# Fourteen like products ahead of the first transposes, two reordered steps, and V's low part split over two places

## The chip, the cores and the metric

The kernel runs on one core of one Trainium2 chip. The metric is the device time of one execution in microseconds. Before the change the median of three runs is 637.38 us (637.07 to 637.69). The profile shows one further execution of 637.08 us, whose span from the first to the last instruction is 635.3 us.

The engines are called by the profile's short names: PE is TensorE (PEld its weight loads), DVE is VectorE, ACT is ScalarE, POOL is GpSimd, SP is SyncE, which here only issues DMAs. ACTq and SPq are DMA issues on ACT's and SP's instruction streams.

## The reference

Decaying linear attention in blocks of 64 rows, then a channel mixer with a low-rank term over the sequence:

```python
# q, k, v: (4, 8, 768, 64); lam: (8,), between 0.97 and 0.99
for b in range(nb):                                   # attention, block = 64
    intra = einsum('bhic,bhjc->bhij', qb, kb) * Dmask # lam**(i-j), lower triangle
    intra = einsum('bhij,bhjd->bhid', intra, vb)
    inter = einsum('bhid,bhde->bhie', qb * lam_pow, kv_state)
    out[:, :, sl] = intra + inter
    kv_state = lam_block * kv_state + einsum('bhsd,bhse->bhde', kb * rev_pow, vb)
x = out.transpose(0, 2, 1, 3).reshape(B, S, H * D)    # (4, 768, 512)
h = x.transpose(0, 2, 1) @ U @ V                      # U: (768, 32), V: (32, 768), float64 inputs
u = x + h.transpose(0, 2, 1)
out = u + maximum(u @ w_ch1, 0) @ w_ch2               # 512 -> 2048 -> 512
```

The float64 inputs U, V and the two mixer weights reach the kernel as pairs of 32-bit words and are turned into float32 on DVE and ACT in small steps.

## The kernel before, in words

**Tiling.** The sequence is taken in 24 steps of 128 rows, six per batch entry (`NS = 24`, `NT = 6`). All eight heads of a step lie side by side in one 128 x 512 tile. Step s loads q, k and v (256 KB each), transposes q and k with PE (`prep`, L419), multiplies them (`scores`, L466), masks the scores with powers of lam (`masked`, DVE, L475), applies them to v (`intra`, L524), adds the part from the running state (`inter`, L536), and updates the state (`state`: products `pkv`, L489, and a DVE sum into `kv`, L495 to L500). ACT copies the transposes out of PSUM (L425), fades the state (L459) and copies the finished rows out (`take_x`, L546). POOL scales k and q by powers of lam (`ks`, L439; `qs`, L450). After six steps `low` (L556) forms the product with U, and from the eighth step on `mix` (L631), `mixed` (L643) and `turn` (L694) apply V to the rows of the batch entry before and transpose them. This front part takes about 112 us; the mixer's large products fill the rest.

**Order of the work.** Nothing is reordered by a scheduler in the front: `pieces` lists the pieces of every step in the order in which each engine gets its instructions, and each engine runs its own list in order, waiting on semaphores. So an instruction that waits holds up everything behind it on its engine. DMA issues sit in the same lists: q, k and the weights on SP, most v loads on ACT. Conversion steps of U, V and the first weights are strewn between the pieces by `aside(s)`; their ACT instructions are put off to the next `late` piece.

**PSUM.** Banks are taken by tag, one buffer each: "pm", "pqk", "pss", "px". A tile of a tag waits until the tile before it under this tag has been read.

**The opening.** While the first loads are on their way PE runs `keep_busy` products on a tile of zeros (L402): two of 128 x 128, then the product that spreads lam over the partitions (`pl`, L852), then two more of 128 x 128 and nine of 16 x 16. DVE copies `pl` to `lamb`, makes the eight masks by scans (L367), the powers for q by four scans (`powers`, L379), and last copies the mask's final column to `rev` (L857), which POOL needs for `ks`.

**The fourth step (s = 3).** At its end `aside(3)` comes ahead of `masked(4)`. It holds four DVE instructions: the last two of U (L196, L201) and the first two of V (L170, L158). V's two ACT instructions (L177, L178) follow in step 4, after the copies of step 5's transposes and ahead of `take_x(4)`.

**The eighth step (s = 7).** `intra(7)` comes ahead of `state(7)`; the state's products use the tag "pqk". Then `inter(7)`, `mix(0)` under the tag "pm", `scores(8)`, and on DVE `mixed(0)`, which `mix(1)` waits for. In the seventh step `aside(6)` puts both halves of V's low part (L799, 32 x 384 each) on DVE, behind `masked(7)`.

## Time and profile before

| what | value |
|---|---|
| three runs | 637.07, 637.38, 637.69 us |
| the profiled execution, and its span | 637.08 us, 635.3 us |
| PE busy | 627.3 us (99% of the span) |
| DVE, ACT, POOL busy | 467.6, 330.9, 146.9 us |
| DMA rate from 6 to 10 us | 280 to 288 GB/s |

PE is busy almost throughout, so the time is the sum of PE's work plus the few places where PE stands idle or runs slowly. To read the profile for this change one looks at those few places in the first 42 us, and asks in each case what was late.

### The profile page before, as it was taken

To read this page: it belongs to the slowest core of one execution; us is meant where nothing else is said; L and a number is where in the kernel's file an instruction comes from. 1 tells how busy PE (TensorE), PEld (TensorE's weight loads), DVE (VectorE), ACT (ScalarE), POOL (GpSimd) and SP (SyncE) were. 2 spreads that over 40 slices of the span, in tenths; PEclk is the share of its full clock that TensorE was granted. 3 is DMA by queue.
4 is the path that set the end of the run, shared out by engine and by line. 5 is a ranking of instruction groups with operands and counts; after the bars stand their busy time and mean duration, and the time that the engine had idled before them with its cause. 6 is when DMAs were issued, how large, how long until landed. Compare 5 with 4: busy or idle time off the path is not lost.

```text
span 635.3 us, 13669 instructions
## 1 busy us (share of the span) xinstructions
PE 627.3 (99%) x5213; PEld 529.2 (83%) x5213; DVE 467.6 (74%) x752; ACT 330.9 (52%) x604; POOL 146.9 (23%) x125
## 2 busy tenths in 40 slices
PE   9999999999999999999999999999999999999997
PEld 8888989888888888888888888888888888888886
DVE  5776887757888788797888799784665754855844
ACT  4675756546777777778777744332322322323220
POOL 4476878000000000000667500030210300300300
PEclk9999999999999999999999999999999999999999
DMA  9989995348797888755876796363353353542521
GB/s 223 254 215 253 249 247 153 133 166 289 284 348 270 309 292 291 272 199 187 262 231 212 239 323 217 116 232 100 108 208 99 137 195 100 190 128 96 183 84 66
DMA packets 141955, 129.61 MB, mean 204 GB/s; under 512 B 82562, under 2 KB 99970, under 8 KB 141890
## 3 DMA queue, kind: packets, MB, share of 16 engines
q1 hardware_dynamic: 116768, 122.32, 59.6%
q10 hardware_dynamic: 25122, 6.42, 4.5%
q8 instruction: 41, 0.67, 0.4%
q14 instruction: 24, 0.20, 0.1%
HBM read 79.04 MB, written 49.28 MB: 202 GB/s over the span
## 4 chain that ended last, share of the span: by engine, by line
PE 97%; DVE 1%; ACT 1%; DMA 1%; issue 0%; ACTq 0%; DVEq 0%
PE pz L983 24%; PE pz L1343 14%; PE pz L1345 14%; PE pd L1347 14%; PE z L983 5%; PE pss L466 4%; PE px L524 4%; PE p L983 3%; PE pz L911 2%; PE d L983 2%; PE px L536 2%; PE pqk L419 2%; PE c L983 2%; PE pkv L489 1%; PE pd L922 1%; PE pp L556 1%
## 5 line engine op out<-in xcount | busy, mean ns | idle before, releaser
L1319 ACT ACTIVATE m<-rm 128x512 fp32r<-128x512 f32 x96 | 60.6, 631 | 174.0 <-PE pd L1347 131.0
L1324 DVE SCALAR_TENSOR_TENSOR m<-rm,m 128x512 fp32r<-128x512 f32 x96 | 71.6, 747 | 81.0 <-ACT m L1319 81.0
L983 PE MATMUL pz<-u_hl,w 128*128 128x512 f32 x448 | 110.3, 389 | 0.0
L1343 PE MATMUL pz<-w_hl,m 128*128 128x512 f32 x264 | 102.7, 389 | 0.0
L1345 PE MATMUL pz<-w_hl,m 128*128 128x512 f32 x264 | 102.7, 389 | 0.0
L1347 PE MATMUL pd<-w_d,m 128*128 128x512 f32 (+1 forms) x267 | 101.4, 387 | 0.0
L983 PEld LDWEIGHTS pz<-u_hl,w 128*128 128x128 f32 x448 | 84.1, 188 | 17.5
L285 POOL TENSOR_TENSOR w<-w 128x512 fp32r<-128x512 f32 x29 | 40.5, 1414 | 210.8 <-DVE w L279 197.3
L1325 DVE SCALAR_TENSOR_TENSOR m<-m 128x512 fp32r<-128x512 f32 x96 | 74.9, 780 | 3.1
L1375 POOL TENSOR_TENSOR o<-o,u 128x512 f32<-128x512 f32 x20 | 29.8, 1521 | 198.5 <-DVE o L1371 198.5
L983 PE MATMUL pz<-u_d,w 128*128 128x512 f32 x224 | 59.9, 389 | 0.0
L1347 PEld LDWEIGHTS pd<-w_d,m 128*128 128x128 f32 x267 | 49.8, 188 | 10.3
L1345 PEld LDWEIGHTS pz<-w_hl,m 128*128 128x128 f32 x264 | 49.6, 188 | 10.3
L1343 PEld LDWEIGHTS pz<-w_hl,m 128*128 128x128 f32 x264 | 49.6, 188 | 10.2
L983 PEld LDWEIGHTS pz<-u_d,w 128*128 128x128 f32 x224 | 42.0, 188 | 8.7
L1343 PE MATMUL pz<-w,m 128*128 128x512 f32 x120 | 46.7, 389 | 0.0
L1345 PE MATMUL pz<-w,m 128*128 128x512 f32 x120 | 46.7, 389 | 0.0
L1347 PE MATMUL pd<-w,m 128*128 128x512 f32 x120 | 46.7, 389 | 0.0
L990 ACT ACTIVATE pz<-pz 128x512 f32<-128x512 f32 x56 | 32.5, 581 | 26.4 <-PE pz L983 26.4
L475 DVE TENSOR_TENSOR sm<-pss,mask 128x512 f32<-128x512 f32 x48 | 30.9, 685 | 18.7 <-PE pss L466 18.4
L994 ACT ACTIVATE r<-pz 128x512 f32<-128x512 f32 x56 | 33.2, 595 | 12.1 <-PE pz L983 11.4
L196 DVE SCALAR_TENSOR_TENSOR sc<-words,sc 128x512 uint32<-128x512 uint32 (+2 forms) x34 | 23.7, 696 | 18.0 <-ACT sc L178 18.0
(140 smaller groups left out, 1119.8 us busy)
## 6 DMA issues: line engine op xcount, KB each, us to landing
r_d<-r SPq DMA_DIRECT2D x96, 256.0 KB, 2.9
rm<-r_d SPq DMA_DIRECT2D x96, 256.0 KB, 2.6
words<-in_moe_w_ch_dram SPq DMA_DIRECT2D x30, 512.0 KB, 5.1
wf<-forms_d SPq DMA_DIRECT2D x56, 128.0 KB, 2.9
u_d<-x_nat SPq DMA_DIRECT2D x24, 256.0 KB, 3.8
u<-u_d SPq DMA_DIRECT2D x24, 256.0 KB, 4.9
qraw<-in_q_dram SPq DMA_DIRECT2D x23, 256.0 KB, 5.0
out_dram<-o SPq DMA_DIRECT2D x23, 256.0 KB, 2.0
```

Source lines behind the costliest of these rows:

```text
L285: engine.tensor_tensor(out=st["third"], in0=st["low"].bitcast(FP32), in1=st["hi"].bitcast(FP32), op=ALU.subtract,)
L475: nc.vector.tensor_tensor(out=sm[:, x], in0=pss[:, x], in1=mask[:, x], op=ALU.mult)
L983: nc.tensor.matmul(out=out, lhsT=weights, rhs=moving, start=start and i == 0, stop=i == len(pieces) - 1, skip_group_check=not start,)
L990: nc.scalar.mul(acc, acc, 1.0 + E)
L994: nc.scalar.mul(r, acc, 4096.0)
L1319: nc.scalar.activation(out=m[:, 0], in_=rs[i], func=AF.Relu, scale=NEAR)
L1324: nc.vector.scalar_tensor_tensor(m[:, 1], r, 0.0, hi, ALU.max, ALU.subtract)
L1325: nc.vector.scalar_tensor_tensor(m[:, 2], hi, E, low, ALU.mult, ALU.subtract)
L1343: nc.tensor.matmul(out=pz, lhsT=m[:, 0, cols], rhs=hi, start=first, stop=False)
L1345: nc.tensor.matmul(out=pz, lhsT=m[:, 1, cols], rhs=low, start=False, stop=end)
L1347: nc.tensor.matmul(out=pd[:, part], lhsT=m[:, 2, cols], rhs=third[:, part], start=first, stop=end, skip_group_check=part.stop != C,)
L1375: nc.gpsimd.tensor_tensor(out=o, in0=o, in1=u, op=ALU.add)
```

## The change

Four things are edited.

1. The opening: the tile of zeros gets ones in its first row (`ones`) and a second zeroed tile (`rows`, 64 columns) takes lam in its first row by a DVE copy. The product that spreads lam then has the same form as the others: 128 x 128 weights, 64 columns moving. The run is 128, 128, 64 columns, lam's 64, and ten of 56 columns: fourteen products on the same weights.
2. `rev` is copied ahead of `powers`. POOL's first `qs` therefore waits for DVE's `powers` by a semaphore of its own.
3. The fourth step: `aside(3)` comes behind `masked(4)` on DVE.
4. The seventh and eighth step: one half of V's low part moves ahead of `masked(7)` (the new piece `v_low`), the other stays behind it. `state(7)` comes ahead of `intra(7)` and uses the tag "pm", the tag that `mix(0)` takes next.

The order of DMA issues on SP and ACT and the order of instructions on POOL stay as they are, as do all later stages.

```diff
-    def keep_busy(n):
+    def keep_busy(sizes):
         out = two_banks("idle", "pm")[:, 0]
-        for i in range(n):
-            k = P if i < 2 else D // 4
+        for n in sizes:
             nc.tensor.matmul(
-                out=out[0:k, 0:k], lhsT=blank[:, 0:k], rhs=blank[:, 0:k], start=True, stop=True
+                out=out[:, 0:n], lhsT=ones, rhs=ones[:, 0:n], start=True, stop=True
             )
...
-                tag = "pm" if s <= NT else "pss" if c > 1 else "pqk"
+                tag = "pm" if s <= NT + 1 else "pss" if c > 1 else "pqk"
...
-        both = [("intra", s), ("state", s)] 
+        both = [("intra", s), ("state", s)] + [("v_low", s)] * (s == NT)
...
-            step += (both if s > NT else both[::-1]) + [("next_v", s), ("inter", s)]
+            step += (both if s > NT + 1 else both[1:] + both[:1]) + [("next_v", s), ("inter", s)]
...
-        aside_first = 0 < s < NT - 2 or s > NT and c > 0
+        aside_first = 0 < s < NT - 3 or s > NT and c > 0
...
-        def low(g, engine):
-            for out, rows in parts((g,)):
+        def low(g, engine, half=slice(0, 2)):
+            for out, rows in list(parts((g,)))[half]:
...
-            five, lambda: low(3, nc.gpsimd), lambda: low(1, nc.vector),
+            five, lambda: v_low.append(lambda: low(1, nc.vector, slice(0, 1))),
+            lambda: low(3, nc.gpsimd), lambda: low(1, nc.vector, slice(1, 2)),
         ]
+
+    v_low = []
+    run["v_low"] = lambda s: v_low.pop()()
...
-        (v_steps(), (1, 1, 3, 4, 4, 4, 4, 5, 6)),
+        (v_steps(), (1, 1, 3, 4, 4, 4, 4, 5, 5, 6)),
...
-    lam_row = consts.tile([1, H + P], FP32, name="lam_row")
-    blank = x_pool.tile([P, C], FP32, tag="x", name="blank")[:, 0:P]
-    nc.vector.memset(blank, 0.0)
-    nc.vector.memset(lam_row[:, H:], 1.0)
+    lam_row = consts.tile([1, H], FP32, name="lam_row")
+    ones = x_pool.tile([P, C], FP32, tag="x", name="ones")[:, 0:P]
+    rows = x_pool.tile([P, C], FP32, tag="x", name="rows")[:, 0:D]
+    nc.vector.memset(ones, 0.0)
+    nc.vector.memset(ones[0:1], 1.0)
+    nc.vector.memset(rows, 0.0)
...
-    pl = two_banks("pl", "pss")[:, 0, 0:H]
-    keep_busy(2)
-    nc.tensor.matmul(out=pl, lhsT=lam_row[:, H:], rhs=lam_row[:, 0:H], start=True, stop=True)
-    keep_busy(3 + 8)
-    nc.vector.tensor_copy(out=lamb, in_=pl)
+    pl = two_banks("pl", "pss")[:, 0, 0:D]
+    keep_busy([P, P, D])
+    nc.vector.tensor_copy(out=rows[0:1, 0:H], in_=lam_row)
+    nc.tensor.matmul(out=pl, lhsT=ones, rhs=rows, start=True, stop=True)
+    keep_busy([56] * 10)
+    nc.vector.tensor_copy(out=lamb, in_=pl[:, 0:H])
     constants()
+    nc.vector.tensor_copy(out=rev, in_=mask[:, :, :, P - 1])
     powers()
-    nc.vector.tensor_copy(out=rev, in_=mask[:, :, :, P - 1])
```

More of the change, by code (lines that the diff above doesn't have):

```diff
@@ L835 @@
     ordered.enter_context(tc.manual_schedule())
-    lam_row = consts.tile([1, H + P], FP32, name="lam_row")
-    blank = x_pool.tile([P, C], FP32, tag="x", name="blank")[:, 0:P]
-    nc.vector.memset(blank, 0.0)
-    nc.vector.memset(lam_row[:, H:], 1.0)
+    lam_row = consts.tile([1, H], FP32, name="lam_row")
[4 more added lines that the diff above has]
+    nc.vector.memset(rows, 0.0)
     set_ends(vp[:, S + C : S + C + 2].bitcast(FP32))
-    nc.scalar.dma_start(out=lam_row[:, 0:H], in_=lam.unsqueeze(0))
+    nc.scalar.dma_start(out=lam_row, in_=lam.unsqueeze(0))
     load_next("q", nc.sync)
```

## The prediction, made before the changed kernel was run

> **What bounds the kernel now.** I read the page first. PE is busy for 99% of the span, and the chain of waits runs through PE almost alone:

> ```profile
> PE 97%; DVE 1%; ACT 1%; DMA 1%; issue 0%; ACTq 0%; DVEq 0%
> ```

> So an edit counts only where PE stands still or runs slowly. For that I took the chain in order of time, 18 to 42 us (start, duration, what). Of the first 42 us it leaves PE in two places that the change touches:

> ```profile
> 19.63 0.23 ACTq L337
> ...
> 25.44 1.19 PE px L524 x32
> ...
> 37.81 0.98 DVE vp L799
> 38.82 1.52 DVE vp L799
> 40.37 0.41 DVE kv L497
> 40.78 0.61 DVE x_nat L643
> 41.44 0.50 PE pm L631 x4
> ```

> The reader is to see that `intra(4)` at 25.44 comes only after other engines' work, and that `mix(1)` at 41.44 comes behind a row of DVE work. The third view is the timeline, which tells what was late:

> ```profile
> 6.62 2.08 PE L466 MATMUL pss<-qt,kt 64*128 64x128 f32 x16
> ...
> 10.86 1.16 PE L466 MATMUL pss<-qt,kt 64*128 64x128 f32 x16
> ...
> 17.06 1.27 POOL L450 TENSOR_TENSOR qs<-qt,powq 128x512 f32<-128x512 f32 x1 [1.49 <-ACT qt L425]
> ...
> 17.40 1.05 DVE L170 TENSOR_SCALAR sc<-words 128x192 uint32<-128x192 uint32 x1
> ...
> 24.06 0.35 DVE L170 TENSOR_SCALAR sc<-words 64x384 uint32<-64x384 uint32 x1
> ...
> 24.61 1.27 DVE L475 TENSOR_TENSOR sm<-pss,mask 128x512 f32<-128x512 f32 x2
> ...
> 25.44 1.19 PE L524 MATMUL px<-vraw,sm 128*64 128x64 f32 x32 [0.71 <-ACT qt L425]
> ```

> Three things are in it. The same 16 score records take 2.08 us at 6.62 and 1.16 at 10.86: PE begins slowly, though the clock column says full from the start. The fourth step's mask (24.61) starts a whole microsecond after its scores ended (22.46 + 1.16 = 23.62), behind L196, L201, L170 and L158; the profile puts the wait of 0.71 down to ACT, but the first half of the mask ends at 24.61 + 0.68 = 25.29, just ahead of 25.44. And L170 takes 1.05 us while POOL's `qs` and `ks` run (17.06 to 19.36) and 0.35 with POOL idle: DVE is held until POOL is through.

> **The sum's base.** Durations are from the profiled execution: 637.08 us, a span of 635.30 and 1.78 around it. The runs' median, 637.38, is 0.30 above it.

> **The opening.** A second memset (0.17, and a semaphore 0.05) moves PE's first product from 1.05 to 1.27. Records of 128 columns follow each other by 0.21 in the timeline; transposes with 128 weight columns and 64 moving, by 0.107 a pair. I take 0.107 for a record of 56 or 64 columns. Then the run is 0.16 to fill, 4 x 0.21, 2 x 0.107, lam's product with its DVE copy and one wait for the bank about 0.6 (as 2.21 to 2.73 before), 20 x 0.107: it ends near 5.2. From above: lam's two records were 0.235 apart, and 20 such would end near 7.8. I take 5.2, since the transposes load as many weight columns. The first k transposes waited for their load until 5.41 anyway, so this costs nothing; that cover is gone from about 5.4 on.

> If the denser run brings PE to full speed by 6.6, the scores gain 0.92 and the next transposes 0.2. Little of it arrives. The second v load was issued at 7.59 and landed 4.7 later, at 12.30; `state(1)`, which needs it, began at 12.45. In step 2 ACT stands until 19.40, behind a v issue (ACTq) that waits for the q load issued at 13.56, landed after 5.8; ACT's copies from there to 22.40 release `scores(4)` at 22.46, whatever PE did before. So at most 0.15 arrives; with a denser DMA queue (the rate sagged to 210 GB/s at 12 us) perhaps 0.25.

> `rev` ahead of `powers` lets POOL's first `ks` start near 6.15 instead of 7.56; lam itself comes about 0.2 later. `powers` (1.37) then runs beside POOL. Before, nothing showed that pair. If the scans are not held, they end by 8.0, and the mask starts no later than before (8.75). If they are held like L170, they wait for the first `ks` to 7.2 and their last for the second `ks` (its load lands at 8.0) to 9.3, and the mask starts at 9.55 for 8.75, of which 0.6 arrives. The rows nearest by their per-partition column, L500 at 13.27 to 13.85 with POOL busy, kept 0.27 each; I take 0, and 0.6 as the bound. Opening: 0, from -0.25 to +0.6.

> **The fourth step.** The mask now starts at 23.67 and ends at 24.95. `state(4)` ends at 24.65, so `intra(4)` starts there and not at 25.44, and its second half no longer waits: 0.9 gained, and `scores(5)` ends at 27.45, the next transposes at 27.95 (their loads landed by 26.6). Now what comes late. L196 starts at 24.87, L201 at 25.26 (they were 0.39 apart). POOL's `qs` wants to start at 25.38, as its ACT copy is not moved, waits for L201 until 25.62 and holds on until about 26.76 (after such a wait at 38.78 it took 1.14). L170 has to wait for it and ends near 27.0; POOL's `ks` follows (0.92), L158 ends near 28.1, the state's sum L497 at 28.6. ACT does V's two (L177, L178, 0.65 each) from 27.0 and only then `take_x(4)` (0.59), to 28.9. `inter(5)` needs that bank and that sum: 28.98. Before it began at 28.76. So the stall moves from 25.4 to 28.0 and the step loses 0.2. Bounds: L170 and L158 at 0.35 as at 24.06 let `inter(5)` begin at 27.98, 0.8 earlier; L201 behind POOL instead of ahead would cost 1.3. I take 0.2, since POOL is running when L170 comes, as at 17.40. SP's queue has nothing in this step's move, and no DMA waits for it.

> **The seventh and eighth steps.** DVE stood idle from 35.48 to 36.49. V's first half fits there: 0.41 after POOL's hold, at the worst 1.26 as the two averaged. `masked(7)` stays at 36.49. `state(7)` (0.47) fills PE's wait before 37.28; `intra(7)` then runs as before to 38.4, `inter(7)` to 39.04 and not 39.79. `mix(0)` now has to wait for the bank "pm", that is for DVE: mask to 37.78, V's second half, held by POOL, to 38.8 to 39.1, L497 0.42. So `mix(0)` is at 39.3 to 39.6 instead of 39.79, its `mixed` ends by 40.5 to 40.8, in time, and `mix(1)` follows `scores(8)` at 40.7 to 41.0 instead of 41.44: 0.45 gained. Bounds: 0.75, and with the first half at 1.26 and the second at 1.52 as at 38.82, a loss of 0.3. POOL's last low part of the mixed rows may start 0.3 later; SP's four copies that follow it are still behind each other, and `mix(0)` needs them near 39.4.

> **The sum.** 637.08 + 0 + 0.2 - 0.45 = 636.83: 636.8 us, 0.1% under the median. Nothing else changes, and the loads from step 5 on land over 3 us ahead of use in the trace (k of step 5 0.8), so a shift goes through to the end.

> **The rivals.**
> - *V's conversion is not held.* For it: the form took 0.35 at 24.06. Against: POOL was idle then. 637.08 - 0.8 - 0.45 = 635.8.
> - *Slow starts are common before, and the change ends them.* For it: the three runs spread over 0.62, and the profiled one is at the low end. Then the runs before lie 0.3 above what I start from, and an earlier v load gains its 0.25 and the eighth step its 0.75: 636.1 or less, about 635.9. Against: loads bound the opening. [...]
> - *The scans are held.* +0.6: 637.4. [...]
> - *Slower: POOL gets ahead of L201.* Place: 25.3 us. L201 is due 0.12 us before `qs`; if it is later than that, L201, L170, L158 and V's two on ACT all move behind `qs` and `ks`, `inter(5)` begins at 30.08 for 28.76: 637.08 + 1.3 - 0.45 = 637.9, slower than before. The opening's 0.6, or the eighth step's bound, on top gives 638.6.
> - *No denser clock.* If PE does not speed up earlier, so that the fourteen products do not do what they could, the sum stays 636.8, since I gave that 0; it has no chance of its own.

> **How the numbers follow.** I call a change of 0.2% (1.27 us: under 636.1 or over 638.65) about what a measurement of this kernel can tell from none. My own case has 0.40 and the scans held 0.12, both inside the bound; V not held 0.22 and slow starts 0.11, both faster; POOL ahead 0.15, which I count as slower, since one more of the bounds above on top carries it past 638.65. Of the 0.52 inside I give 0.04 to a loss that none of them names. That makes faster 0.33, within 0.48, slower 0.19. The range leaves out the two ends: 635.5, just under the case of V not held, to 638.3, over POOL ahead.

> **What would show it.** Right: the mask of step 4 starting near 23.7 and `intra(4)` near 24.7; L170 near 25.65 with over 1 us; a new PE stall ahead of `inter(5)` near 28 to 29; `mix(0)` waiting for DVE and `mix(1)` with no wait, 0.4 earlier relative to `scores(7)`; the first scores near 1.1 us, and `state(1)` still near 12.4. Wrong: L170 at 0.35 beside POOL, or no stall at 28 (faster); the mask of step 0 after 9.3, or L201 over 1 us (slower); the ten products more than 0.15 apart.

## The result, and the profile after

The changed kernel takes 641.11 us (median; 639.83 to 642.16) beside 637.15 for the kernel before (six executions each): a ratio of 1.0064, 95% interval 1.005 to 1.0078, slower by some 4 us. The profiled execution took 640.86 us with a span of 639.08 (before 637.08 and 635.30).

By engine, the chain of waits of the changed kernel is still PE's:

```profile
PE 97%; DVE 1%; issue 0%; ACT 0%; ACTq 0%; DVEq 0%
```

The same chain in order of time (start, duration, what) answers the lines shown of before. "issue" is time in which PE waited for nothing that the profile shows:

```profile
3.27 4.25 PE idle L401 x20
...
8.88 2.08 PE pss L465 x16
...
28.20 1.33 DVE u_w L201
29.55 1.11 DVE sc L170
30.68 0.62 ACT sc L177
...
31.85 0.57 ACT x_nat L545
...
32.51 0.69 PE px L535 x32
...
35.39 1.29 PE pp L555 x38
36.68 1.00 issue
37.68 0.62 PE pp L555 x10
...
42.95 1.24 DVE vp L798
...
44.71 0.57 PE pm L630 x4
```

Four things are to be seen. The opening's twenty records of 56 columns stand on the chain themselves, up to 7.52. `intra(4)` has no wait any more, but L201 takes 1.33 us and behind it a row of conversions makes `inter(5)` late (32.51). A stall of 1.00 us cuts the product with U after 38 of its 48 records. And `mix(0)` waits for DVE (44.71) while `mix(1)` follows without a wait. The timeline tells why L201 is long: POOL's `qs` (L449) began 0.38 ahead of it, and beside it L201 takes 1.32 us, for 0.36 before. Before, the four scans, L201 and `qs` read so:

```profile
6.04 1.37 DVE L379 TENSOR_TENSOR_SCAN powq<-small 128x128 f32<-128x128 f32 x4
...
23.67 0.36 DVE L201 SCALAR_TENSOR_TENSOR u_w<-m,sc 128x192 f32<-128x192 f32 x1
...
25.38 1.28 POOL L450 TENSOR_TENSOR qs<-qt,powq 128x512 f32<-128x512 f32 x1 [2.11 <-ACT qt L425]
```

After:

```profile
3.06 4.46 PE L401 MATMUL idle<-ones 128*128 128x56 f32 x20
...
6.50 2.26 POOL L438 TENSOR_TENSOR ks<-kraw,small 128x512 f32<-128x512 f32 x2 [5.19 <-DVE small L862]
...
6.71 2.97 DVE L379 TENSOR_TENSOR_SCAN powq<-small 128x128 f32<-128x128 f32 x4
...
8.88 2.08 PE L465 MATMUL pss<-qt,kt 64*128 64x128 f32 x16 [0.31 <-ACT kt L424]
...
13.59 1.16 PE L465 MATMUL pss<-qt,kt 64*128 64x128 f32 x16
...
27.82 1.48 POOL L449 TENSOR_TENSOR qs<-qt,powq 128x512 f32<-128x512 f32 x1 [2.86 <-ACT qt L424]
28.20 1.32 DVE L201 SCALAR_TENSOR_TENSOR u_w<-m,sc 128x192 f32<-128x192 f32 x1
...
29.55 1.10 DVE L170 TENSOR_SCALAR sc<-words 64x384 uint32<-64x384 uint32 x1
```

Reading the start of the same work in both timelines shows where the time goes. From the first product of the mixer (L911; L917 after) to the end, all twenty traces of this study take 522.40 to 522.47 us, so only the front differs:

| starts at (us) | before | after | difference |
|---|---|---|---|
| `scores(0)` | 6.62 | 8.88 | +2.26 |
| `scores(1)` | 10.86 | 13.59 | +2.73 |
| `scores(4)` | 22.46 | 25.11 | +2.65 |
| `scores(5)` | 27.18 | 29.19 | +2.01 |
| `scores(6)` | 30.47 | 34.22 | +3.75 |
| `scores(7)` | 35.28 | 40.43 | +5.15 |
| `scores(9)` | 44.84 | 49.48 | +4.64 |
| mixer's first product | 112.89 | 116.66 | +3.77 |

The opening costs 2.26 and a further 0.47 because PE becomes fast later (at 12.45, for 9.03 before). The fourth step wins 0.64 and loses 1.74, the product with U loses 1.40, the seventh and eighth win 0.51. The last 0.87 comes back: 0.64 of it in short stalls, of which before has 0.92 in this stretch (0.15, 0.20 and 0.57) and after 0.28.

### The profile page after: what moved, and what is told of

Its sections match the earlier page's. It is cut to its first block, busy times and chain, and to the rows that moved or that the text cites. A ratio compares the mean times of both kernels' runs of the same rounds, so it can differ in the third digit from the quotient of the medians.

```text
span 639.1 us, 13671 instructions
## 1 busy us (share of the span) xinstructions
PE 630.3 (99%) x5213; PEld 532.8 (83%) x5213; DVE 472.6 (74%) x754; ACT 330.8 (52%) x604; POOL 147.5 (23%) x125
## 4 chain that ended last, share of the span: by engine, by line
PE 97%; DVE 1%; issue 0%; ACT 0%; ACTq 0%; DVEq 0%
PE pz L989 24%; PE pz L1351 14%; PE pz L1349 14%; PE pd L1353 14%; PE z L989 5%; PE pss L465 4%; PE px L523 4%; PE p L989 3%; PE pz L917 2%; PE d L989 2%; PE px L535 2%; PE pqk L418 2%; PE c L989 2%; PE pkv L488 1%; PE pd L928 1%; PE pm L630 1%
## 5 line engine op out<-in xcount | busy, mean ns | idle before, releaser
L285 POOL TENSOR_TENSOR w<-w 128x512 fp32r<-128x512 f32 x29 | 40.5, 1414 | 210.8 <-DVE w L279 193.8
L1000 ACT ACTIVATE r<-pz 128x512 f32<-128x512 f32 x56 | 33.2, 595 | 12.0 <-PE pz L989 11.4
L196 DVE SCALAR_TENSOR_TENSOR sc<-words,sc 128x512 uint32<-128x512 uint32 (+2 forms) x34 | 23.8, 699 | 16.7 <-ACT sc L178 16.6
```

The lines of the kernel that those rows point to most:

```text
L285: engine.tensor_tensor(out=st["third"], in0=st["low"].bitcast(FP32), in1=st["hi"].bitcast(FP32), op=ALU.subtract,)
L1000: nc.scalar.mul(r, acc, 4096.0)
```

## The experiments

Each kernel was timed in a set, beside the kernel before on the same chip; the sets ran on several chips. "us" is the ratio less 1, times 637. The expectations quote differences of medians instead, which differ a little.

| kernel | ratio to before | 95% interval | us |
|---|---|---|---|
| opening alone | 1.0032 | 1.0019 to 1.0045 | +2.0 |
| fourth step alone | 1.0044 | 1.0026 to 1.0062 | +2.8 |
| eighth step alone | 0.9989 | 0.9972 to 1.0007 | -0.7 |
| `rev` alone | 0.9991 | 0.9982 to 1.0001 | -0.6 |
| changed, old opening | 1.0055 | 1.0034 to 1.0076 | +3.5 |
| changed, old fourth step | 1.002 | 1.0005 to 1.0034 | +1.3 |
| changed, narrow weights | 1.0066 | 1.0045 to 1.0086 | +4.2 |
| changed, without the ten | 1.0017 | 1.0 to 1.0035 | +1.1 |
| opening alone, narrow | 1.0009 | 0.9997 to 1.0021 | +0.6 |
| fourth step, 24 records more | 1.0052 | 1.0034 to 1.0071 | +3.3 |
| fourth step, 16 records fewer | 1.0013 | 0.9995 to 1.0031 | +0.8 |
| fourth step, split | 0.9991 | 0.9979 to 1.0003 | -0.6 |
| changed, again | 1.0078 | 1.0064 to 1.0092 | +5.0 |
| changed, three repairs | 1.0005 | 0.9994 to 1.0016 | +0.3 |
| eighth step, dense old opening | 1.0 | 0.9985 to 1.0014 | 0 |
| eighth step and `rev` | 0.9994 | 0.998 to 1.0007 | -0.4 |
| eighth step and split | 1.0 | 0.9983 to 1.0017 | 0 |
| eighth step, split and `rev` | 1.0004 | 0.9993 to 1.0014 | +0.3 |

### The parts alone

The opening alone, with `rev`, the fourth and the eighth step as before:

```diff
-    keep_busy(2)
-    nc.tensor.matmul(out=pl, lhsT=lam_row[:, H:], rhs=lam_row[:, 0:H], start=True, stop=True)
-    keep_busy(3 + 8)
+    keep_busy([P, P, D])
+    nc.vector.tensor_copy(out=rows[0:1, 0:H], in_=lam_row)
+    nc.tensor.matmul(out=pl, lhsT=ones, rhs=rows, start=True, stop=True)
+    keep_busy([56] * 10)
...
```

> The kernel before with the fourteen like products alone (the order of rev and powers, the fourth and the eighth step as before). Theory A, the products cost the time: twenty records of 56 columns at 0.21 us, the run ends near 7.5 and not 4.4, the first scores start near 8.9 for 6.6, and everything up to scores(4) is 2.3 to 2.8 us late: +2.5 us, 639.6. Theory B, the opening is bound by the loads and the loss comes from the reordered steps: the first scores are late, but state(1) and scores(4) catch up with their loads, at most +0.4 us, 637.5. Theory C, the loss lies in PE's instruction stream (a stall of 1.0 us marked issue at 37.7 in the changed kernel): +1.0 us or less, with such a stall near 37.

Theory A held, with 2.0 us for its 2.5. In its trace the first scores start at 8.88 as in the changed kernel, and `scores(4)` at 24.81 (changed 25.11, before 22.46); by `scores(7)` (36.80) only 1.5 is left, because `intra(4)` no longer finds DVE late when PE itself is late.

The eighth step alone:

```diff
-                tag = "pm" if s <= NT else "pss" if c > 1 else "pqk"
+                tag = "pm" if s <= NT + 1 else "pss" if c > 1 else "pqk"
...
-        both = [("intra", s), ("state", s)] 
+        both = [("intra", s), ("state", s)] + [("v_low", s)] * (s == NT)
...
```

> The kernel before with the eighth step's order, the tag pm and V's low part in two places alone. Theory A: mix(1) comes 0.45 us earlier than before, and the end with it: -0.45 us, 636.7, between -0.3 and -0.75. Theory B, the reordered steps cost the time: +0.5 us or more. Theory C: the order of PE's instructions moves its stalls marked issue, so that the difference is anything between -1.0 and +1.0 while mix(1) is 0.4 earlier against the scores before it.

Its median agreed, but its interval includes no change, and its trace does not show the gain: `scores(7)` to `scores(9)` takes 10.39 us, for 9.56 before, because three of the four records of `mix(0)` wait for a copy of rows of the product with U that landed late:

```profile
40.70 0.50 PE L631 MATMUL pm<-vp 64*128 64x256 f32 x3 [1.43 <-DMA vp<-vp]
```

The trace of `rev` alone, with the old eighth step, has the same wait (1.07; 10.64 us), so this edit alone does not make it; why these copies land late is not known. In the eleven other traces with the new eighth step the stretch takes 9.05 to 9.19 us, in the other seven without it 9.45 to 9.82: a gain of about 0.4, which the trace of the eighth step alone does not have.

The fourth step alone:

```diff
-        aside_first = 0 < s < NT - 2 or s > NT and c > 0
+        aside_first = 0 < s < NT - 3 or s > NT and c > 0
```

> The kernel before with the conversion steps behind the fourth step's mask alone. Theory A: POOL's qs begins ahead of L201, which takes over 1 us, inter(5) starts about 1.0 to 1.3 us later than before and so does the end: +1.0 us, 638.2. Theory B, L201 still comes ahead of qs without the late opening: +0.2 us, 637.4, with L201 at 0.36. Theory C as for the others: stalls marked issue move, and with them the end.

More than expected. Its chain of waits shows both losses of the changed kernel, and a third:

```profile
21.86 0.92 PE pss L466 x10
22.78 0.51 issue
23.30 0.55 PE pss L466 x5
...
25.63 1.32 DVE u_w L201
...
32.81 1.29 PE pp L556 x37
34.09 1.05 issue
35.14 0.63 PE pp L556 x11
```

The changed kernel with the old opening, `rev` alone, and the changed kernel with the old fourth step:

> The changed kernel with the opening's products as before (rev ahead of powers, the fourth and the eighth step as changed). Theory A: the fourth step's +1.0 and the eighth's -0.45 remain, +0.6 us against the kernel before, 637.7, and 3.4 us less than the changed kernel. Theory B: the loss stays, 640 to 641. Theory C: the stall of 1.0 us near 37 stays at the same place in PE's list, and the time is 638.5 to 639.

> The kernel before with rev copied ahead of powers alone. With the old opening the first scores end near 8.1 to 8.7, so the four scans, held beside POOL's two ks (2.9 us in the run with the old opening, against 1.37), end near 9.1 and the first mask waits for them. Theory A: the mask starts 0.6 to 1.0 us after its scores where it started 0.05 after before, and the end is +0.6 us, 0.1%. Rival: loads of the next steps (v of step 1) bind anyway, 0.0 to +0.2 us.

> The changed kernel with the fourth step's conversion steps back ahead of the mask. Theory A: L201 takes 0.36 us again, inter(5) and the product with U follow without the stalls of 1.6 and 1.0 us, and the time is 2.3 us below the changed kernel's: +1.7 us against the kernel before, or less. Rival, the late opening alone decides and the fourth step's stalls are waits that would come elsewhere: +3 to +4 us.

With the old opening 3.5 us remain, as theory B says and far from theory A's 0.6: its trace shows the fourth step's losses, and the scans, held for 2.93 us, keep the first mask until 9.09, 1.0 us after its scores. The profiled execution (639.17) is one of the four faster ones; six others took 640.5 to 643.5, and what they lose is not known. Without the fourth step 1.3 remain, so that step costs 2.8 here as it does alone. `rev` alone costs nothing that can be measured. The four parts alone add up to 2.0 + 2.8 - 0.7 - 0.6 = 3.5 us, for 4.1 and, in a second set, 5.0 together.

### What the opening's records cost

The ten products on 56 weight columns, nothing else changed:

```diff
-                out=out[:, 0:n], lhsT=ones, rhs=ones[:, 0:n], start=True, stop=True
+                out=out[0:n, 0:n], lhsT=ones[:, 0:n], rhs=ones[:, 0:n], start=True, stop=True
```

> The changed kernel with the ten products of 56 columns on 56 weight columns instead of 128; nothing else. Theory W, the load of 128 weight columns sets the spacing of 0.21 us: it falls to about 0.21 x 56 / 128 = 0.09, the run ends near 5.2, the first scores start near 6.6 and the time is 1.9 us below the changed kernel's, which is about +2.1 us against the kernel before. Rival M, the columns moving (or a fixed price of a record) set it: the spacing stays 0.21, the run ends near 7.5, and the time is that of the changed kernel, +4.0 us.

Theory W was right about the records and wrong about the time. Its timeline:

```profile
3.48 1.96 PE L401 MATMUL idle<-ones 128*56 128x56 f32 x20
6.57 1.27 PE L465 MATMUL pss<-qt,kt 64*128 64x128 f32 x16 [0.49 <-ACT kt L424]
6.78 2.22 POOL L438 TENSOR_TENSOR ks<-kraw,small 128x512 f32<-128x512 f32 x2 [5.47 <-DVE small L862]
6.98 2.94 DVE L379 TENSOR_TENSOR_SCAN powq<-small 128x128 f32<-128x128 f32 x4
9.84 1.26 DVE L474 TENSOR_TENSOR sm<-pss,mask 128x512 f32<-128x512 f32 x2
10.55 1.28 PE L523 MATMUL px<-vraw,sm 128*64 128x64 f32 x32 [1.55 <-DVE sm L474]
```

While PE is slow its records start 0.0933 us apart, and with 128 weight columns 0.2133 us: 0.0933 is 0.2133 x 56 / 128. So the number of weight columns sets the pace of these products, and on 128 of them a record with 56 moving columns takes as long as one with 128 (0.213 and 0.214 us in the trace of the changed kernel). The rest of the lines shows what took the gain: the scans, held beside POOL's two `ks` (2.94 for 1.37 before), keep the first mask until 9.84, and PE waits 1.55 us for the first mask. That was hidden in the changed kernel only because its scores came so late. The fourth step's stalls are there too, and in three of the six executions the mean granted clock is 0.996 to 0.997 (641.8 to 643.3 us; the others 639.5 to 640.0), for which the last section shows a possible cause.

The ten products left out, and the narrow form with the old order of `rev`, the old fourth and the old eighth step:

> The changed kernel without the ten products of 56 columns, so that PE's run of like products ends near 3.3 and its instructions come 40 places earlier in its stream. If the length of the run costs the time, the first scores start near 6.6, 1.9 us below the changed kernel, +2.1 us against the kernel before, and the first mask waits for the held scans as in the run with the old opening. If the ten products bring the clock up, the granted clock rises a window (3.4 us) later than in the changed kernel and the time is no better, +4.0. If the stall of 1.0 us marked issue in the product with U comes from the place in the stream, it moves 20 products later in PE's list.

> The kernel before with the like products alone, as in the run of the opening alone (+1.9 us), but the ten products of 56 columns on 56 weight columns; rev, the fourth and the eighth step as before. If the weight load's 0.21 us a record is what the opening costs, the run ends near 5.3, the scores start near 6.6 as before and the +1.9 us is gone: -0.5 to +0.5 us. If lam's later arrival (its DVE copy, 0.48 us later to lamb) or the place in PE's stream costs the time, +1 us or more stays.

Left out, 3 us of the changed kernel's loss go, 1.0 more than the opening costs alone; the stall in the product with U is gone as well (below). But its executions scatter from 636.0 to 641.1, and the profiled one (639.89) reaches the mixer's first product at 115.63, as late as the run with narrow weights; what the faster ones win is not shown. The clock rose at 11.3, and in the changed kernel at 12.45: without the ten it rises sooner, and not the expectation's 3.4 us later (the rises of before and after, 9.03 and 12.45, lie that far apart). Narrow and with `powers` ahead of `rev`, the opening costs 0.6 us with an interval that includes none, for 2.0 with wide weights: the width of the weights is most of it.

Dense products in the old opening, for an earlier clock:

```diff
-            k = P if i < 2 else D // 4
+            k = P if i < 2 else 56
...
-    keep_busy(3 + 8)
+    keep_busy(2 + 7)
```

> The kernel before with the eighth step's edits (-1.0 us when alone) and in the old opening seven products of 56 x 56 in place of nine of 16 x 16, so that PE computes densely from 1.05 to about 4.9 and lam's product keeps its old form. If density brings the clock up, as in the run with narrow weights (rise at 5.1 us), it rises a window of 3.4 us earlier in most executions, the first scores take less than 2.1 us, and the time is 0.5 to 1.0 us below the run of the eighth step alone: -1.5 to -2.0 us, 635.6 to 636. If the loads bind, -1.0 us as without it.

The clock did rise early (6.37 us, for 9.03 in the trace of before) and the first scores took 1.27, but nothing of it arrives: `prep(2)` then waits 0.23 for its q load and `state(1)` 0.19 for v. There the loads do bind.

### What the fourth step costs

The conversions split: U's two stay ahead of the mask, V's two go behind it.

```diff
+        step += [("aside", s + 0.5)] * (s == NT - 3)
...
-        (v_steps(), (1, 1, 3, 4, 4, 4, 4, 5, 6)),
+        (v_steps(), (1, 1, 3.5, 4, 4, 4, 4, 5, 6)),
```

> The kernel before with only V's two conversion steps (L170, L158) behind the fourth step's mask; U's two (L196, L201) stay ahead of it. Theory R, the race of L201 against POOL's qs costs the step: L201 is 0.36 again, V's L170 is still held by qs (over 1 us), ACT's two follow from about 26.7 and inter(5) starts near 28.8 as before; the time is 0 to +0.3 us. Theory H, V's conversions held by POOL and the late copies on ACT cost it, whichever comes first: +0.8 us or more. Theory F, any step that makes inter(5) wait moves the fetch of PE's instructions and costs about 1 us on top: +1 to +2 us.

Theory R held: -0.6 us, from -1.3 to +0.2. POOL still holds one of V's conversions, but it is the second (L158, 1.43 us for 0.35 before), so that ACT gets its input at 26.1 instead of 28.1, and `inter(5)` does not wait:

```profile
25.73 0.34 DVE L170 TENSOR_SCALAR sc<-words 64x384 uint32<-64x384 uint32 x1
25.73 1.47 POOL L450 TENSOR_TENSOR qs<-qt,powq 128x512 f32<-128x512 f32 x1 [2.35 <-ACT qt L425]
25.99 1.43 DVE L158 TENSOR_SCALAR m<-words 64x384 uint32<-64x384 uint32 x1
```

In the six traces in which L201 comes behind `qs` (changed, changed again, fourth alone, old opening, narrow weights, without the ten), `scores(5)` to `scores(6)` takes 5.02 to 5.03 us, for 3.29 before: 1.74 lost each time. In all six ACT copies `qt` 0.54 to 0.66 us after the mask has started, so that POOL is ready when the mask ends, before L201's turn comes. The order of the instructions alone does not decide this: in the two runs that follow, with the same order, ACT copies `qt` 1.10 and 2.13 us after the mask's start, and L201 comes ahead of `qs` (0.36 us).

The place in PE's instruction stream, moved by 24 records up and 16 down with the same work:

```diff
-    keep_busy(3 + 8)
+    keep_busy(3 + 20)
```

```diff
-    keep_busy(3 + 8)
+    keep_busy(3)
```

> The run of the fourth step alone (+2.3 us) with twelve more products of 16 x 16 in the opening, 24 records more ahead of everything in PE's stream, which takes 0.65 us of PE's wait for the k load. Theory F, the stall of 1.0 us in the product with U and the 0.5 us in scores(4) come from a fetch of PE's instructions that lands late: they stay at the same places counted in PE's instructions, so 24 records earlier in the work, or go, since the next fetch then falls due ahead of inter(5)'s wait and lands in it; without them the time is +0.9 to +1.3 us against the kernel before. Rival, they belong to the product with U and to scores(4) themselves (late data, the loads): same work, same stalls, +2.3 us or more.

> The run of the fourth step alone (+2.3 us) with eight fewer products of 16 x 16 in the opening, 16 records fewer ahead of everything. Theory F: the stalls at scores(4) and in the product with U come 16 records later in the work or are gone, as in the run without the ten products, and the time is +0.9 to +1.5 us. Rival, the stalls belong to the work: +2.3 us as before.

With 16 fewer the cost falls from 2.8 to 0.8 us, with an interval that includes none. Part of this is the race: a stall of 1.38 us makes ACT copy `qt` late, L201 takes 0.36, and `scores(5)` to `scores(6)` takes 3.29 as before. So the fall does not price the stalls by themselves. Its chain shows that the stall of `scores(4)` stays at its place in the stream and so hits other work: there it came after 10 records of the scores, here after the scores' 16 and 9 of the transposes behind them, 15 records later by the trace, in which a record can be missing.

```profile
23.21 1.09 PE pss L466 x16
24.30 0.29 PE pqk L419 x9
24.60 1.38 issue
25.98 0.40 PE pqk L419 x7
```

So these stalls belong to PE's instruction stream and not to the work. Counting PE's weight loads and waits in its own list, the stalls marked issue that are longer than 0.14 us start at the same counts, to within one, and a multiple of about 130 apart; left out are nine at the first product of `intra(7)` or `inter(5)`, which need the result of another engine. Some of them, with their lengths in us:

```
count    360   491   621   751  1270  1399  1528  2047  2305
before     -     -     -     -  0.15  0.20     -     -  0.57
after      -     -     -  1.00     -     -  0.28     -     -
again      -     -     -  0.45     -  0.30     -  0.69     -
fourth     -  0.51     -  1.05     -     -  0.82     -     -
fewer      -  1.38     -     -     -     -     -     -  0.43
none       -     -     -     -  0.60     -     -  0.81     -
split   0.55  0.27  0.34     -     -  0.36     -     -     -
```

The table of DMA queues names a queue for instructions:

```profile
q8 instruction: 41, 0.67, 0.4%
```

With 24 more the trace shows L201 ahead of `qs` (0.36 us), a wait of only 0.46 before `inter(5)`, and no stall in the product with U, as theory F says:

```profile
25.46 0.36 DVE L201 SCALAR_TENSOR_TENSOR u_w<-m,sc 128x192 f32<-128x192 f32 x1
25.63 1.32 POOL L450 TENSOR_TENSOR qs<-qt,powq 128x512 f32<-128x512 f32 x1 [2.15 <-ACT qt L425]
25.85 1.31 DVE L170 TENSOR_SCALAR sc<-words 64x384 uint32<-64x384 uint32 x1
```

In this trace `scores(4)` to `scores(6)` takes 8.13 us for 8.01 before, close to the 0.2 that the prediction had for this step: with L201 ahead its account holds. Yet the time is +3.3, as the rival says. The profiled execution (638.87) is the fastest of its six (the others 640.35 to 642.14), so it may not stand for them; what they lose is not known.

### The whole again, and mended

> The changed kernel itself, a second time, beside the other runs of this set: +4.0 us against the kernel before. If L201 behind POOL and the stall of 1.0 us in the product with U are fixed to the order of the work, its trace shows both again (L201 at 1.3 us, the wait of 1.6 us before inter(5), the stall in the product with U); if they are scatter of one execution, one of them is missing.

Both findings recur: L201 1.32 us, `inter(5)` 1.66 late, the stall at count 751, now 0.45. With 5.0 us this set is dearer than the first.

Three repairs of the changed kernel: the ten products narrow, `powers` ahead of `rev`, and U's conversions ahead of the mask as in the split.

> The changed kernel with three repairs: the ten products on 56 weight columns, U's two conversions back ahead of the fourth step's mask with V's two behind it, powers ahead of rev. If the weight load and the race are the whole loss, +0.6 (the narrow opening) -0.9 (the eighth step) + 0 to 0.3 (the split): about 0 against the kernel before. If more than 1.5 us is left, a third cause is missing.

They take the whole loss away: +0.3 us, from -0.4 to +1.0. With the eighth step's gain of about 0.4 counted back, no further loss of the 1.5 us that the expectation names is left. Stalls marked issue remain in its trace (0.76 and 0.55 us), as they do before.

Could what is left beat the kernel before?

> The kernel before with the eighth step's edits and rev ahead of powers, each of which gave -0.85 to -0.95 us alone, with an interval that just reached zero. If both are gains they add: -1.8 us, 635.7. If the gain of rev was scatter of the clock's start, -1.0 us; if both were, 0.

> The kernel before with the eighth step's edits and with V's two conversion steps (not U's) behind the fourth step's mask. Alone they gave -1.0 and -0.6 us, each with an interval past zero. If both are gains that add: -1.6 us, 635.8. If the executions' scatter (start of the clock, fetch stalls) made them: 0.

> The same with rev copied ahead of powers, which gave -0.85 us alone and next to nothing beside the eighth step. If it is a gain: -2.2 us or less; if not, as without it, or +0.3 us where the held scans let the first mask wait.

No. None of the three is measurably faster; the gains of the single parts, whose intervals all reached past zero, do not add. Where they went is only partly known: in the trace of the eighth step and the split, `scores(7)` to `scores(9)` takes 9.16 us for 9.56 before, so the eighth step's 0.4 is there, but one stall at count 1528 takes 1.30. No kernel found here beats the one before.

## Why the prediction was wrong, by its own steps

Predicted were 636.8 us (635.5 to 638.3), measured 641.1. Two terms of the sum failed: the opening, put at 0, costs 2.0 us alone, and the fourth step, put at 0.2, costs 2.8 alone, of which stalls marked issue, that no term contained, are a part.

**What bounds the kernel: right.** All the difference lies where PE stands or runs slowly in the front, and the 522.4 us behind it never move.

**The opening: wrong, a mis-sized term.** The prediction took 0.107 us for a record of 56 columns, from transposes that "load as many weight columns". But 0.107 is the price of a pair of those, whose loads are 64 rows high, and it is one of transposes. The score records, products of 64 rows with 128 weight columns, come in pairs every 0.213 us at 6.62 in the trace of before, and were the nearer row; why transposes run at twice their pace no run separates. Measured for the ten products: 0.2133 a record. Its own upper bound, an end "near 7.8", was close to the 7.5 found, yet no price was put on it: the sum said that loads bind up to `scores(4)` whatever PE does. They bind a PE that is early (the dense opening showed that); here v landed at 11.9 and `state(1)` began at 15.17. A cover for a gain was taken as a cover for a loss. Term: 0 (up to +0.6), measured +2.0.

**The clock: the wrong sign.** The denser run was to bring full speed forward or do nothing; that density brings it forward was the author's guess, which no row of before shows. The trace's record of the granted clock begins, at full clock, at 9.03 before and 12.45 after, 3.42 us later; for the time ahead of it the profile's clock column shows 1.00, which is why the prediction read "full from the start" there. PE's pace changes at these times: before, pairs of transposes follow at 0.107 us up to 9.03 and at 0.063 from there; after, pairs of state products at 0.107 up to 12.45 and pairs of `intra(0)` at 0.058 from there. Over all traces this rise lies at 8.3 to 11.6 with the old opening, at 10.9 to 13.7 with ten wide products, at 11.3 without them, and at 5.1 to 6.4 (once 11.4) with narrow ones. The first scores took 2.08 as before, not 1.1.

**`rev` and `powers`: right, both ways.** The scans are held (2.97 for 1.37), one of the two cases named. Two of the four scans take 1.16 and 1.25 us, each beside one of POOL's two `ks`, and the others 0.39, for 0.40 to 0.43 before. L201 shows the same in the trace of before: in the form of 128 x 512 it takes 1.51 us at 85.08, beside POOL, and 0.69 at 114.95 without. The taken price of 0 also stands, but for reasons not foreseen: in the changed kernel the late scores hide it, alone the scans end at 8.34, just as the scores do, and with early scores (the narrow run) it costs 1.55.

**The fourth step: the named rival came in.** L201 was put 0.12 us ahead of `qs`, by taking ACT's copy of `qt` from the trace of before, where ACT was late: at 24.74 it lay 1.07 behind the mask's new start. In the changed kernel it came 0.55 behind. So POOL won. The rival's price was 1.3 for `inter(5)`; measured 1.74 less the 0.64 won ahead of it, 1.1. The rival had been given a chance of 0.15, though everything hung on a margin smaller than the shift of ACT. V's L170 held beside POOL, the point of the step's main case, was right (1.10).

**What no step contained: the stalls marked issue.** The stall of 1.00 us makes the product with U lose 1.40, with the slow records around it. Before has such stalls too (0.15, 0.20, 0.57), and the prediction did not read them; that moving waits moves these stalls was not considered.

**The eighth step: right.** Predicted 0.45; `scores(7)` to `scores(9)` takes 9.05 and 9.07 in the two traces of the changed kernel, 9.56 before: 0.5. `mix(0)` waits for DVE and `mix(1)` for nothing, as described. As a gain in time it is not shown: the interval alone includes none, and one trace lacks it.

Of the signs named for "wrong", the three for slower came: products more than 0.15 apart, L201 over 1 us, and the mask of step 0 after 9.3 (11.01), this one for the late scores and not for the scans.

## What to carry to other kernels

Price a filler product by its weights as well as by its moving columns: here a record of 56 columns took 0.213 us on 128 weight columns and 0.093 on 56, and behind the ten wide ones the clock rose at 12.45, for 9.03 before. Where two engines hold each other up (L201 beside `qs` took 1.32 us for 0.36, and `qs` 1.48 for 1.28) and one is due only a tenth of a microsecond ahead, the order of the instructions does not decide which comes first; keep the one that others wait for out of the race. A transfer that hides a gain says nothing about a loss.

## What the runs showed that was not expected

**A busy PE is not enough for the clock.** Between 4 and 8 us the changed kernel's PE shows 4.00 busy of 4.00 us, with wide records of 56 columns to 7.5 and transposes after, and still the clock rose only at 12.45. With narrow records, as many columns in less than half the time, it rose at 5.13 and 5.95, but with the three repairs only at 11.35. The stretches at full clock that begin with the rise last 624.64, 628.05 or 631.47 us in the traces (and 20.48 in one), whole multiples of 3.413. Counted back from 12.45 in steps of 3.413, the one from 2.2 to 5.62 had PE busy throughout, and no rise came at its end. So PE's busy time in the profile does not tell when the clock rises; what does is not shown.

**After one stall PE ran 3.42 us at half clock.** In the trace of the narrow opening alone, a stall of 1.51 us at 24.0 leaves PE busy for 1.84 of 3.41 us, and the next 3.42 us run at a granted clock of 0.50 (columns: window; length; busy time of PE, PEld, DVE, ACT, POOL; granted clock; DMA share; GB/s):

```profile
23.02:26.43 3.41, 1.84 (x32) 1.65 (x32) 1.60 (x5) 2.37 (x8) 0.88 (x1) 1.00 1.05 235
26.43:29.85 3.42, 3.42 (x72) 3.19 (x71) 1.44 (x3) 2.19 (x4) 2.29 (x2) 0.50 0.84 190
```

`intra(4)` took 1.92 us in it, for 1.19 before. That the stall is the cause is an inference from this one trace. Its execution took 639.45 us beside a median of 637.82 for that kernel; executions with a mean clock of 0.996 to 0.997 are found for other kernels as well.
